# Attention and feed-forward on one core: the hand-written order redone from tile 0's last chunks on, with part of VectorE's work on GpSimd

## The chip, the cores and the metric

The kernel runs on one core of a Trainium2 chip. The metric is device time in microseconds (us) of one execution. Each time given for a kernel is the median of its runs. The traces come from one profiled execution each.

A core has five engines with an instruction queue each: TensorE (PE) multiplies matrices, VectorE (DVE), ScalarE (ACT) and GpSimd (POOL) work element by element, and SyncE (SP) issues transfers. Each engine runs its queue strictly in program order. An instruction that waits for another engine or a transfer holds up all that is queued behind it.

## The reference

Causal linear attention with a decay per head, and behind it a SwiGLU feed-forward block. B=4, H=8, S=768, D=64; 3072 tokens of width 512; the inner width d_ff is 1536. All inputs and the output are fp32.

```python
for b in range(nb):                       # blocks of 64 positions, state kv carried along
    intra = einsum('bhic,bhjc->bhij', qb, kb) * Dmask
    intra = einsum('bhij,bhjd->bhid', intra, vb)
    inter = einsum('bhid,bhde->bhie', qb * lam_pow, kv_state)
    out[:, :, sl] = intra + inter
    kv_state = lam_block * kv_state + einsum('bhsd,bhse->bhde', kb * rev_pow, vb)
x = out.transpose(0, 2, 1, 3).reshape(3072, 512)
g = x @ w_gate
result = (g * sigmoid(g) * (x @ w_val)) @ w_out
```

## The kernel before

Matmuls run in bf16. The attention works in 12 **groups** g, each one batch and a pair of blocks of 128 positions, all heads. Two groups make a **tile** t of 512 tokens, and there are six tiles for the feed-forward. The inner width is cut into 12 chunks fc of 128.

What a group goes through, with the names of the helpers and the lines on which they issue:
- `load_fp32` fetches k, q and v (L109; from group 6 on L116 and L124, in four pieces for q and for k and two for v). SP issues these transfers.
- `kcast` (L278) and `qcast` (L282, it also multiplies the decay in) write k and q as bf16 into one tile `qk`; `v_scale` (L260) does the same for v, with the decay factors.
- `dma_transpose` (L268) turns the whole `qk` into `qkt` by a transfer on SP. It needs both casts. From group 3 on all groups use it.
- `scores` (L347, from group 6 on L383) and `mask` (L358, L362, on DVE) make the block's own weights; `intra` (L554) and `inter` (L541) make the output in a pair of PSUM banks, from the block and from the state; `guard` (L525) reads that pair on ACT between the two; `evr` (L569, L572) copies it to `xt`, the input of the feed-forward.
- `upd_mm` (L408) makes the update of the state from k and v. `sadd` (L489), `kvm` (L508), `kv0c` (L513), `kvf0`, `kvz` and `kvn` (L443, L445) add it, decay it and copy it to bf16 for the next blocks.

The feed-forward: tiles 0 to 2 take `ffn_gate` (L600, with silu on ACT in L605) and `ffn_val` (L618, with the product on DVE in L622) for a chunk and all or half of the tile's tokens. Tiles 3 to 5 use Strassen's method in Winograd's form: `unit` holds six PSUM banks, `uprod` (L755) is one of its seven products for gate or value, with sums on ACT and DVE (L759 to L765), then `silu` (L774) and `mu` or `mup` (L780). The sums of weights and inputs that it needs come from `w_combo` (L680) and `x_combo` (L719). The last product takes `ffn_out` for tile 0, and for the other tiles `oprod` (L814, sums in L817 to L829), seven products likewise, whose sums of inputs come from `hsum` (L673) and `wo_combo` (L658). `wo_cast` (L254) makes bf16 of w_out.

The order on every engine is written out by hand as a list of several hundred such calls; there is no scheduler (`tc.manual_schedule()`). The arguments name the engine where there is a choice (`nc.gpsimd` or `POOLC` is POOL, `nc.vector` or `DVEC` is DVE, `ACTC` is ACT), and `use(...)` names the PSUM banks (0 to 7) that the next call takes. A call whose bank is still being read waits. From the list, around the first changed place:

```python
    kcast(3)
    qcast(3, nc.gpsimd)
    dma_transpose(3)
    load_fp32(4, nc.sync, v, "v")
    use(6); ffn_gate(0, 11, 2, 4)
    use(7); ffn_val(0, 11, 2, 4)
    v_scale(3, nc.gpsimd)
    v_scale(4, nc.gpsimd)
```

The arguments of a matmul call are the tile, the chunk and the half of the tile's tokens (`0, 2` or `2, 4`; `0, 4` is the whole).

Of the kernel before, what the change touches and what calls it, by code (L numbers as in the profile page):

```python
# [37 lines left out]
def _body(ctx, tc, nc, q, k, v, lam, moe_w_gate, moe_w_val, moe_w_out, out):  # L38
# [896 lines left out]
    def use(*bk):  # L935
        fixed[:] = bk
# [40 lines left out]
    use(2, 3, 4, 5); scores(2)  # L977
    mask(2, 0, 0)
    mask(2, 0, 1)
    mask(2, 1, 0)  # L980
    mask(2, 1, 1)
    use(6); ffn_gate(0, 10, 0, 4)
    use(7); ffn_val(0, 10, 0, 4)
    use(0); ffn_gate(0, 11, 0, 2)
    use(1); ffn_val(0, 11, 0, 2)
    use(2, 3); upd_mm(2)
    kvz(2)
    kvf0(2)
    use(4, 5); op_bare(2)
# [3 lines left out]
    evr(2, 0, DVEC)  # L993
    evr(2, 1, ACTC)
    sadd(2, 1)
# [12 lines left out]
    new_xt(2)  # L1008
    use(0); ffn_gate(1, 0, 0, 2)
    use(1); ffn_val(1, 0, 0, 2)  # L1010
    use(2); ffn_gate(1, 1, 0, 2)
    use(3); ffn_val(1, 1, 0, 2)
    use(4); ffn_gate(1, 2, 0, 2)
    use(5); ffn_val(1, 2, 0, 2)
    use(6); ffn_gate(1, 3, 0, 2)
    use(7); ffn_val(1, 3, 0, 2)
    kcast(4)
    qcast(4, nc.vector)
# [8 lines left out]
    use(0); ffn_gate(1, 4, 0, 2)  # L1027
    use(1); ffn_val(1, 4, 0, 2)
    use(2); ffn_gate(1, 5, 0, 2)
    use(3); ffn_val(1, 5, 0, 2)  # L1030
    use(4); ffn_gate(1, 6, 0, 2)
    use(5); ffn_val(1, 6, 0, 2)
    use(6); ffn_gate(1, 7, 0, 2)
    use(7); ffn_val(1, 7, 0, 2)
    use(0, 1, 2, 3); scores(3)
    use(4, 5); upd_mm(3)
    mask(3, 0, 0)
    mask(3, 1, 1)
    mask(3, 0, 1)
    mask(3, 1, 0)  # L1040
    use(2, 3); op_new(3)
    kvz(3)
    use(6); ffn_gate(1, 8, 0, 2)
    use(7); ffn_gate(1, 9, 0, 2)
    use(0); ffn_gate(1, 10, 0, 2)
    inter(3, True)
    guard(3)
    use(6); ffn_gate(1, 11, 0, 2)
    kvf0(3)
    intra(3, False)  # L1050
    use(0, 6); upd_mm(4)
    sadd(3, 1)
    sadd(4, 0)
    use(1); ffn_val(1, 10, 0, 2)
    evr(3, 1, ACTC)
    evr(3, 0, ACTC)
    use(4); ffn_val(1, 11, 0, 2)
    kvm(3, nc.vector)
    use(5); ffn_val(1, 8, 0, 2)
    use(7); ffn_val(1, 9, 0, 2)  # L1060
    use(3); ffn_gate(1, 0, 2, 4)
    kcast(5, ACTC)
    use(5); ffn_gate(1, 1, 2, 4)
    qcast(5, nc.vector)
    use(0); ffn_gate(1, 2, 2, 4)
    kvn(4, 0, ACTC)
    use(7); ffn_gate(1, 3, 2, 4)
    sadd(4, 1)
    use(1); ffn_val(1, 0, 2, 4)
    use(3); ffn_val(1, 1, 2, 4)  # L1070
    use(5); ffn_gate(1, 4, 2, 4)
    use(4); ffn_gate(1, 5, 2, 4)
    kvm(4, nc.vector)
    use(2); ffn_val(1, 2, 2, 4)
    use(7); ffn_val(1, 3, 2, 4)
    use(1); ffn_gate(1, 6, 2, 4)
    use(5); ffn_val(1, 6, 2, 4)
    use(6); ffn_gate(1, 7, 2, 4)
    use(1); ffn_val(1, 5, 2, 4)
    use(4, 3, 2, 6); scores(4)  # L1080
    mask(4, 0, 0)
    mask(4, 1, 0)
    v_scale(5, nc.gpsimd)
    wo_cast()
    wo_cast()
# [4 lines left out]
    use(0, 7); op_new(4)  # L1090
    inter(4, True)
    mask(4, 0, 1)
    use(1); ffn_val(1, 4, 2, 4)
    mask(4, 1, 1)
    use(4); ffn_gate(1, 8, 2, 4)
    guard(4)
    use(5); ffn_gate(1, 9, 2, 4)
    use(2); ffn_gate(1, 10, 2, 4)
    use(4); ffn_val(1, 10, 2, 4)
    use(1); ffn_val(1, 8, 2, 4)  # L1100
    intra(4, False)
    use(4, 2); upd_mm(5)
    new_xt(3)
    evr(4, 0, ACTC)
    evr(4, 1, ACTC)
    use(6); ffn_val(1, 7, 2, 4)
    sadd(5, 0)
    use(3); ffn_val(1, 9, 2, 4)
    use(0); ffn_gate(1, 11, 2, 4)
    kvn(5, 0, ACTC)  # L1110
    use(1); ffn_gate(2, 6, 0, 2)
    wo_cast()
    wo_cast()
    wo_cast()
    sadd(5, 1)
    use(5); ffn_gate(2, 7, 0, 2)
    use(6); ffn_val(1, 11, 2, 4)
    use(4); ffn_val(2, 6, 0, 2)
    wo_cast(ACTC)
    use(7); ffn_out(0, 0)  # L1120
    use(6); ffn_gate(2, 8, 0, 2)
    wo_combo(0)
    wo_combo(1)
    w_combo(0, 0, (0, 3))
    w_combo(1, 0, (0, 3))
    kvm(5, nc.vector)
    use(2); ffn_val(2, 8, 0, 2)
    use(7); ffn_val(2, 7, 0, 2)
    use(4); ffn_gate(2, 9, 0, 2)
    use(3); ffn_out(0, 1)  # L1130
    kcast(6, ACTC)
    qcast(6, nc.gpsimd)
    use(0, 2); op_new(5)
    use(7, 5, 4, 6); scores(5)
    inter(5, True)
    dma_transpose(6)
    load_fp32(7, nc.sync, k, "kraw")
# [40 lines left out]
    out_new(1, (0,), [4, 6, 0], 0)  # L1178
    mask(6, 0, 1)
    use(5); ffn_val(2, 9, 2, 4)  # L1180
    sadd(6, 0)
    w_combo(0, 1, (0, 3))
    mask(6, 0, 0)
    oprod(1, 0, 1)
    kv0c(5, ACTC)
    use(5); ffn_gate(2, 10, 0, 4)
    oprod(1, 0, 7)
    kvn(6, 0, ACTC)
    sadd(6, 1)
    oprod(1, 0, 6)  # L1190
    kvn(6, 1, ACTC)
    sadd(6, 2)
    use(2); ffn_gate(2, 11, 0, 4)
    kvn(6, 2, ACTC)
    sadd(6, 3)
    use(1); ffn_val(2, 8, 2, 4)
    w_combo(1, 1, (0, 3))
    oprod(1, 0, 5)
    oprod(1, 0, 2)
    use(2); ffn_gate(2, 0, 0, 4)  # L1200
    use(3); ffn_val(2, 0, 0, 4)
    use(1); ffn_val(2, 11, 0, 4)
    w_combo(0, 3, (0, 3))
    w_combo(0, 2, (0, 3))
    use(5); ffn_val(2, 10, 0, 4)
    oprod(1, 0, 3)
    use(4); ffn_gate(2, 1, 0, 4)
    oprod(1, 0, 4)
    store(1, 0, 1, 0, 512, None)
    store(1, 0, 0, 0, 512, None)  # L1210
    use(1, 3); op_new(6)
    inter(6, True)
    use(2, 5); upd_mm(7)
    use(6, 4); scores(7)
    guard(6)
    intra(6, False)
    w_combo(1, 2, (0, 3))
    evr(6, 1, ACTC)
    kcast(8, ACTC)
    mask(7, 0, 0)  # L1220
    hsum(1, 1, 0, 6, 1, 2, nc.vector)
    mask(7, 0, 1)
    use(7); ffn_val(2, 1, 0, 4)
    sadd(7, 0)
    kvm(6, nc.vector)
# [5 lines left out]
    out_new(1, (1,), [0, 7, 4], 0)  # L1231
    kv0c(3, ACTC)
    use(3); ffn_gate(2, 2, 0, 4)
    evr(6, 0, ACTC)
    use(6); ffn_gate(2, 3, 0, 4)
    oprod(1, 1, 1)
    use(3); ffn_val(2, 2, 0, 4)
    kvn(7, 0, ACTC)
    sadd(7, 1)
    oprod(1, 1, 7)  # L1240
    kvn(7, 1, ACTC)
    sadd(7, 2)
    oprod(1, 1, 6)
    oprod(1, 1, 2)
    kvn(7, 2, ACTC)
    use(1); ffn_gate(2, 4, 0, 4)
    oprod(1, 1, 4)
    sadd(7, 3)
    v_scale(8, nc.vector, 0, 4)
    v_scale(8, nc.gpsimd, 4, 8)  # L1250
    w_combo(1, 3, (0, 3))
    kvm(7, nc.vector)
    oprod(1, 1, 5)
    use(4, 3); op_new(7)
    inter(7, True)
    use(5, 2); upd_mm(8)
    use(1, 0); scores(8)
    mask(8, 0, 1)
    sadd(8, 0)
    guard(7)  # L1260
    intra(7, False)
    evr(7, 1, ACTC)
    evr(7, 0, ACTC)
    kv0c(4, ACTC)
    kv0c(6, ACTC)
    kvn(8, 0, ACTC)
    sadd(8, 1)
    kvn(8, 1, ACTC)
    use(6); ffn_gate(2, 5, 0, 4)
    v_scale(9, nc.gpsimd, 0, 4)  # L1270
    sadd(8, 2)
    x_combo(3, 0, None, nc.vector)
    x_combo(3, 1, None, nc.vector)
    x_combo(3, 3, None, nc.vector)
    use(0); ffn_val(2, 4, 0, 4)
    mask(8, 0, 0)
    x_combo(3, 2, None, nc.vector)
    use(5); ffn_val(2, 3, 0, 4)
    kvn(8, 2, ACTC)
    hs_new(2)  # L1280
    new_xt(4)
    unit(3, 0, (2, 4, 3, 1, 6, 5))
    uprod(3, 0, 0, 0)
    uprod(3, 0, 1, 0)
    kcast(9, ACTC)
    uprod(3, 0, 0, 1)
    oprod(1, 1, 3)
    uprod(3, 0, 1, 1)
    uprod(3, 0, 3, 0)
    silu(3, 0, 0, 0)  # L1290
    qcast(9, nc.vector)
    uprod(3, 0, 2, 0)
    use(0); ffn_val(2, 5, 0, 4)
# [5 lines left out]
    use(2, 0); op_new(8)  # L1299
    uprod(3, 0, 2, 1)  # L1300
    uprod(3, 0, 4, 0)
    uprod(3, 0, 5, 0)
    inter(8, True)
    uprod(3, 0, 3, 1)
    mu(3, 0, 0, 0)
    hsum(2, 0, 0, 4, 0, 2, nc.vector)
    uprod(3, 0, 6, 0)
    guard(8)
    silu(3, 0, 1, 1)
    silu(3, 0, 1, 0)  # L1310
    silu(3, 0, 0, 1)
# [417 lines left out]
```

## Time and profile before

| | |
|---|---|
| time, median of 3 runs | 214.70 us (214.65 to 215.71) |
| the profiled execution | 215.46 us, of which its trace spans 213.5 us |
| granted TensorE clock in it | 0.998 of full speed |
| instructions | 6988 |

The trace covers 213.5 of the profiled execution's 215.46 us; the rest lies before the first instruction and behind the last. In the profile's rows a line such as L282 is the line of the helper that issued the instruction, so one line stands for all groups and a row's start tells which group it is. In a timeline, a row gives the start in us, the duration in us, engine, line, operation, output and input by the program's names, and how many instructions of one kind stand in it; the bracket at the end is the engine's idle time just before it and what ended that. SPq and POOLq are the queues of these engines, with the transfers that they issue.

### The profile page before, as it was taken

How to read it: one execution, taken by the hardware profiler on the slowest of the kernel's cores; microseconds unless marked ns; L12 is line 12 of the kernel's file. 1: busy time of each engine (PE TensorE's matmuls, PEld its weight loads, DVE VectorE, ACT ScalarE, POOL GpSimd, SP SyncE). 2: the span in 40 equal slices, each digit the busy share in tenths (PEclk: the TensorE clock that was granted, in tenths of full speed). 3: DMA queues.
4: the chain of work that ended last, by engine and by line, in shares of the span. 5: the costliest groups of instructions: out<-in, count | busy, mean ns of one | idle time of the engine just before them, and what ended most of it. 6: DMA issues, size and time to landing. Idle time of an engine off the chain costs nothing.

```text
span 213.5 us, 6988 instructions
## 1 busy us (share of the span) xinstructions
PE 206.1 (97%) x2873; PEld 160.4 (75%) x2873; DVE 158.7 (74%) x304; ACT 133.1 (62%) x287; POOL 72.4 (34%) x92
## 2 busy tenths in 40 slices
PE   8799999999999999999899999999999999999993
PEld 3466455888886648876667888888888888888883
DVE  1774447678678898986898999979896779953960
ACT  6888575656635444838578986657763577527522
POOL 6685755705362030640103289802000000006600
PEclk9999999999999999999999999999999999999999
DMA  6999999989999967999777858972000500005014
GB/s 189 344 354 382 377 355 282 306 224 250 284 392 156 225 195 166 267 171 226 204 198 173 196 128 197 274 219 107 5 3 0 196 3 0 3 0 196 3 51 147
DMA packets 82177, 39.77 MB, mean 186 GB/s; under 512 B 45410, under 2 KB 77794, under 8 KB 82146
## 3 DMA queue, kind: packets, MB, share of 16 engines
q1 hardware_dynamic: 80946, 38.74, 66.4%
q10 hardware_dynamic: 1200, 0.59, 0.9%
q8 instruction: 22, 0.36, 0.7%
q14 instruction: 9, 0.07, 0.1%
HBM read 28.31 MB, written 6.29 MB: 162 GB/s over the span
## 4 chain that ended last, share of the span: by engine, by line
PE 68%; SPq 13%; DMA 10%; POOL 3%; issue 2%; ACT 2%; DVE 1%; POOLq 0%; DVEq 0%
PE bank L755 25%; PE bank L814 17%; PE bank L600 10%; PE bank L618 10%; DMA qraw<-in_q_dram 6%; SPq L124 6%; DMA v<-in_v_dram 3%; SPq L116 3%; SPq L109 3%; POOL qk L282 2%; SPq L268 2%; PE bank L554 2%; PE bank L541 1%; PE bank L408 1%; POOL v_s L260 1%
## 5 line engine op out<-in xcount | busy, mean ns | idle before, releaser
L622 DVE TENSOR_TENSOR h<-sil,bank 128x256 bf16<-128x256 bf16 (+1 forms) x55 | 26.9, 500 | 17.4 <-PE bank L618 13.1
L618 PE MATMUL bank<-xt,wv_sb 128*128 128x256 bf16 (+1 forms) x228 | 38.4, 301 | 0.1
L600 PE MATMUL bank<-xt,wg_sb 128*128 128x256 bf16 (+1 forms) x228 | 38.2, 301 | 0.0
L605 ACT ACTIVATE sil<-bank 128x256 bf16<-128x256 f32 (+1 forms) x55 | 24.5, 451 | 18.2 <-PE bank L600 14.8
L260 POOL TENSOR_TENSOR v_s<-v,dec 128x512 bf16<-128x512 f32 (+1 forms) x15 | 19.8, 1328 | 36.1 <-DMA v<-in_v_dram 35.9
L618 PEld LDWEIGHTS <-wv_sb 128*128 128x128 bf16 x228 | 21.8, 98 | 9.3 <-issue 0.4
L600 PEld LDWEIGHTS <-wg_sb 128*128 128x128 bf16 x228 | 21.7, 98 | 8.5 <-issue 0.2
L814 PEld LDWEIGHTS <-h 128*128 128x128 bf16 x240 | 23.4, 98 | 4.6 <-issue 1.1
L755 PEld LDWEIGHTS <-ws 128*128 128x128 bf16 x216 | 20.9, 98 | 3.1 <-issue 0.5
L814 PE MATMUL bank<-wo_sb,h 128*128 128x256 bf16 x180 | 22.4, 273 | 0.0
L755 PE MATMUL bank<-xs,ws 128*128 128x256 bf16 x144 | 20.7, 272 | 0.2 <-ACT bank L759 0.2
L780 DVE TENSOR_TENSOR h<-sil,bank 128x512 bf16<-128x512 bf16 x27 | 18.2, 681 | 1.8 <-PE bank L755 1.5
L814 PEld LDWEIGHTS <-hs 128*128 128x128 bf16 x180 | 17.6, 98 | 2.2
L774 ACT ACTIVATE sil<-bank 128x512 bf16<-128x512 f32 x27 | 15.7, 594 | 5.2 <-PE bank L755 5.0
L673 POOL TENSOR_TENSOR hs<-h,hs 128x512 bf16<-128x512 bf16 x2 | 2.3, 1152 | 46.4 <-DVE hs L673 46.3
L362 DVE TENSOR_TENSOR ssb<-bank,causal 128x512 bf16<-128x512 f32 x24 | 15.2, 682 | 2.0 <-PE bank L347 1.2
L763 DVE TENSOR_TENSOR bank<-bank,es 128x512 f32<-128x512 f32 x18 | 12.3, 696 | 5.9 <-PE bank L755 5.5
L755 PE MATMUL bank<-xt,wg_sb 128*128 128x256 bf16 x108 | 15.9, 273 | 0.2 <-DVE kvf L489 0.2
L755 PE MATMUL bank<-xt,wv_sb 128*128 128x256 bf16 x108 | 16.1, 273 | 0.0
L755 PEld LDWEIGHTS <-wg_sb 128*128 128x128 bf16 x144 | 14.0, 98 | 2.3 <-issue 0.4
L814 PE MATMUL bank<-wt,hs 128*128 128x256 bf16 x120 | 15.5, 272 | 0.0
L755 PEld LDWEIGHTS <-wv_sb 128*128 128x128 bf16 x144 | 13.9, 98 | 1.7
(133 smaller groups left out, 373.4 us busy)
## 6 DMA issues: line engine op xcount, KB each, us to landing
out_dram<-osb SPq DMA_DIRECT2D x22, 256.0 KB, 2.3
v<-in_v_dram SPq DMA_DIRECT2D x18, 256.0 KB, 4.6
woraw<-in_moe_w_out_dram SPq DMA_DIRECT2D x6, 512.0 KB, 7.7
kraw<-in_k_dram SPq DMA_DIRECT2D x24, 128.0 KB, 3.6
qraw<-in_q_dram SPq DMA_DIRECT2D x24, 128.0 KB, 3.4
wraw<-in_moe_w_gate_dram SPq DMA_DIRECT2D x5, 512.0 KB, 6.9
wraw<-in_moe_w_val_dram SPq DMA_DIRECT2D x5, 512.0 KB, 6.8
kraw<-in_k_dram SPq DMA_DIRECT2D x4, 512.0 KB, 6.6
```

The source lines that it names most:

```text
L124: eng.dma_start(out=t[p0:p0 + n, :, s * D:s * D + D], in_=bass.AP(tensor=src.tensor, offset=base + (H - 1) * S * D * rev + (p0 + s * BLK) * D,
L260: eng.tensor_tensor(out=st[("vs", g)][:, h0:h1], in0=st[("v", g)][:, h0:h1].rearrange("p h (s d) -> p h s d", s=2), in1=vfac(g, h0, h1), o ...
L362: nc.vector.tensor_tensor(out=st[("ssb", g)][:, h2, 2 * c:2 * c + 2].rearrange("p a s n -> p a (s n)"), in0=st[("sp", g, c, h2)].rearrange ...
L600: nc.tensor.matmul(gp[:, n0:n1], wg_sb[:, mc, fs], xt[:, g0:g1, mc].rearrange("p g b n -> p g (b n)"), start=(mc == 0 and n0 == 0), stop=( ...
L605: nc.scalar.activation(sil[:, 0:N], gp[:, 0:N], AF.Silu)
L618: nc.tensor.matmul(vp[:, n0:n1], wv_sb[:, mc, fs], xt[:, g0:g1, mc].rearrange("p g b n -> p g (b n)"), start=(mc == 0 and n0 == 0), stop=( ...
L622: nc.vector.tensor_tensor(out=h_sb[:, fc % FH, b0:b1].rearrange("p b n -> p (b n)"), in0=sil[:, 0:N], in1=vp[:, 0:N], op=ALU.mult)
L755: nc.tensor.matmul(o[i][:, fi * 256:fi * 256 + 256], lhs(c, 2 * j + fi), rhs(c), start=(k < 2 and fi == 0 and c == 0), stop=(c == KH - 1), ...
L763: nc.vector.tensor_tensor(out=E[i], in0=Bb[i], in1=es[i], op=ALU.add)
L774: nc.scalar.activation(sil[half, r], unit_src(t, j, half, r)[0], AF.Silu)
L780: eng.tensor_tensor(out=st[("h", t, half)][:, 2 * j:2 * j + 2][:, :, r:B:2], in0=v3(st[("u", t, j)][4][half, r]), in1=v3(unit_src(t, j, ha ...
L814: nc.tensor.matmul(o, lhs(f), rhs(f), start=(k in (1, 7) and f == 0), stop=(f == FH - 1), skip_group_check=True)
```

## The change

The list of calls is written anew from tile 0's last three chunks on, up to some way into unit (5,2) of the last tile; the calls behind that and the helpers are the same. The same matmuls are issued, in another order and with other PSUM banks. SP issues the same transfers in the same order. On the engines:
- From DVE to POOL: `qcast(4)`, `qcast(5)`, `kvm(3)` to `kvm(7)`, `v_scale(6)`, half of `v_scale(8)`, half of `v_scale(11)`, five `x_combo` (of tiles 3, 4 and 5), four `mup` (of units (4,0) to (5,0)) and several `hsum` of tiles 2 to 4; two `hsum` go the other way.
- Between ACT and POOL: `kv0c(2)` and `kvn(11,1)` to ACT, or back to it; `kcast(10)`, `kvn(6,1)` and `kvn(8,1)` to POOL.
- `qcast` of groups 3, 6, 7, 10 and 11 is on POOL in both kernels, and that of 8 and 9 on DVE in both.

In the diff, cut to the parts around groups 3 to 5, around groups 8 and 9, and one of the later parts:

```diff
     kcast(3)
+    use(3); ffn_val(1, 0, 0, 2)
+    use(0); ffn_gate(1, 3, 0, 2)
+    v_scale(3, nc.gpsimd)
     qcast(3, nc.gpsimd)
     dma_transpose(3)
     load_fp32(4, nc.sync, v, "v")
-    use(6); ffn_gate(0, 11, 2, 4)
-    use(7); ffn_val(0, 11, 2, 4)
-    v_scale(3, nc.gpsimd)
...
+    use(7, 0); upd_mm(3)
...
+    kcast(4)
...
+    qcast(4, nc.gpsimd)
+    kvm(2, nc.gpsimd)
+    kvm(3, nc.gpsimd)
     v_scale(4, nc.gpsimd)
-    kvm(2, nc.gpsimd)
-    kv0c(2, POOLC)
     load_fp32(5, nc.sync, k, "kraw")
     load_fp32(5, nc.sync, q, "qraw")
...
-    qcast(4, nc.vector)
+    use(3, 0); op_new(3)
+    inter(3, True)
+    use(4, 7, 2, 1); scores(3)
...
     v_scale(5, nc.gpsimd)
     wo_cast()
-    wo_cast()
+    qcast(5, nc.gpsimd)
     dma_transpose(5)
     load_fp32(6, nc.sync, k, "kraw")
     load_fp32(6, nc.sync, q, "qraw")
...
     kcast(7, POOLC)
+    kvm(4, nc.gpsimd)
+    kvm(5, nc.gpsimd)
     qcast(7, nc.gpsimd)
...
     qcast(8, nc.vector)
     dma_transpose(8)
     load_fp32(9, nc.sync, k, "kraw")
     load_fp32(9, nc.sync, q, "qraw")
     load_fp32(9, nc.sync, v, "v")
...
+    oprod(1, 1, 6)
...
-    use(4, 3); op_new(7)
+    use(2, 1); op_new(7)
     inter(7, True)
-    use(5, 2); upd_mm(8)
-    use(1, 0); scores(8)
+    guard(7)
+    use(5, 6); scores(8)
+    use(7, 0); upd_mm(8)
+    intra(7, False)
...
+    kcast(9, ACTC)
...
+    use(6); ffn_val(2, 3, 0, 4)
...
-    use(7, 4); upd_mm(9)
-    use(3, 6); scores(9)
+    use(7, 0); upd_mm(9)
+    evr(8, 0, ACTC)
+    evr(8, 1, ACTC)
     uprod(3, 0, 5, 1)
...
+    use(1, 3); scores(9)
...
-    kcast(10, ACTC)
-    qcast(10, nc.gpsimd)
+    kcast(10, POOLC)
+    qcast(10, nc.gpsimd)
```

More of the change, by code (lines that the diff above doesn't have):

```diff
@@ new lines, in _body @@
+    hsum(1, 0, 0, 6, 1, 2, nc.vector)
+    use(1); ffn_val(2, 7, 0, 2)
+    oprod(1, 0, 1)
+    evr(5, 1, ACTC)
+    oprod(1, 0, 7)
+    use(4); ffn_gate(2, 9, 0, 2)
+    w_combo(0, 1, (0, 3))
+    oprod(1, 0, 6)
+    hsum(1, 2, 0, 6, 1, 2, nc.vector)
+    use(1); ffn_gate(2, 6, 2, 4)
+    hsum(1, 3, 0, 6, 1, 2, nc.vector)
+    use(2); ffn_val(2, 9, 0, 2)
+    use(4); ffn_gate(2, 7, 2, 4)
+    oprod(1, 0, 4)
+    use(1, 4); upd_mm(6)
+    use(2, 3); scores(6)
+    sadd(6, 0)
+    use(5); ffn_val(2, 6, 2, 4)
@@ L1209, in _body @@
+    use(5); ffn_gate(2, 1, 0, 4)
+    use(5, 3); op_new(6)
+    kvm(6, nc.gpsimd)
+    v_scale(7, nc.gpsimd)
+    v_scale(8, nc.gpsimd, 0, 4)
+    v_scale(8, nc.gpsimd, 4, 8)
+    use(6); ffn_val(2, 11, 0, 4)
+    inter(6, True)
+    guard(6)
+    use(2, 7); upd_mm(7)
+    use(1, 0); scores(7)
+    intra(6, False)
     store(1, 0, 1, 0, 512, None)
     store(1, 0, 0, 0, 512, None)
[L1211 to L1216, printed above, removed]
@@ L1217, in _body @@
-    w_combo(1, 2, (0, 3))
+    evr(6, 0, ACTC)
+    sadd(7, 0)
+    mask(7, 0, 0)
+    out_new(1, (1,), [6, 4, 5], 0)
+    oprod(1, 1, 1)
+    kcast(8, ACTC)
+    use(1); ffn_gate(2, 2, 0, 4)
+    oprod(1, 1, 7)
+    kvn(7, 0, ACTC)
+    w_combo(0, 3, (0, 3))
+    sadd(7, 1)
+    kvn(7, 1, ACTC)
     evr(6, 1, ACTC)
-    kcast(8, ACTC)
-    mask(7, 0, 0)
-    hsum(1, 1, 0, 6, 1, 2, nc.vector)
+    w_combo(0, 2, (0, 3))
     mask(7, 0, 1)
-    use(7); ffn_val(2, 1, 0, 4)
-    sadd(7, 0)
-    kvm(6, nc.vector)
+    sadd(7, 2)
@@ L1280, in _body @@
+    use(5); ffn_val(2, 5, 0, 4)
     hs_new(2)
     new_xt(4)
-    unit(3, 0, (2, 4, 3, 1, 6, 5))
+    unit(3, 0, (7, 0, 1, 2, 3, 5))
+    uprod(3, 0, 0, 1)
+    use(4); ffn_val(2, 4, 0, 4)
+    use(6); ffn_val(2, 3, 0, 4)
+    qcast(9, nc.vector)
     uprod(3, 0, 0, 0)
+    kv0c(7, ACTC)
     uprod(3, 0, 1, 0)
-    kcast(9, ACTC)
-    uprod(3, 0, 0, 1)
-    oprod(1, 1, 3)
     uprod(3, 0, 1, 1)
+    uprod(3, 0, 2, 0)
+    uprod(3, 0, 3, 1)
+    uprod(3, 0, 2, 1)
     uprod(3, 0, 3, 0)
     silu(3, 0, 0, 0)
-    qcast(9, nc.vector)
@@ L1292, in _body @@
-    uprod(3, 0, 2, 0)
-    use(0); ffn_val(2, 5, 0, 4)
+    uprod(3, 0, 4, 0)
+    mu(3, 0, 0, 0)
+    v_scale(9, nc.gpsimd, 0, 4)
     v_scale(9, nc.gpsimd, 4, 8)
```

724 lines of the change are left out of this document (337 added, 387 removed).

## The prediction

> **What bounds the kernel now.** I read the page first, then TensorE's timeline, then the chain of waits.
>
> ```profile
> span 213.5 us, 6988 instructions
> PE 206.1 (97%) x2873; PEld 160.4 (75%) x2873; DVE 158.7 (74%) x304; ACT 133.1 (62%) x287; POOL 72.4 (34%) x92
> ```
>
> TensorE (PE) is busy for 206.1 of 213.5 us. The change issues the same matmuls, so it can only win what PE loses, some 7 us, much of it ahead of the first redone statement. PE's timeline shows what is lost behind that. Matmul rows overlap, so I measure from one row's start to the next one's start.
>
> ```profile
> 97.93 1.89 PE L600 MATMUL bank<-xt,wg_sb 128*128 128x512 bf16 x8
> 99.65 0.82 PE L814 MATMUL bank<-wo_sb,h 128*128 128x256 bf16 x6
> ...
> 103.13 1.03 PE L600 MATMUL bank<-xt,wg_sb 128*128 128x512 bf16 x4
> 105.02 0.81 PE L814 MATMUL bank<-wt,h 128*128 128x256 bf16 x6 [0.86 <-DVE bank L823]
> ...
> 106.78 0.44 PE L408 MATMUL bank<-v_s,qk 64*64 64x64 bf16 x24
> 107.15 0.44 PE L383 MATMUL bank<-qkt 64*64 64x64 bf16 x32
> ...
> 108.67 2.14 PE L618 MATMUL bank<-xt,wv_sb 128*128 128x512 bf16 x8
> 110.64 1.04 PE L755 MATMUL bank<-xt,wg_sb 128*128 128x256 bf16 x8
> ...
> 114.00 1.03 PE L618 MATMUL bank<-xt,wv_sb 128*128 128x512 bf16 x4
> 115.20 1.03 PE L755 MATMUL bank<-xs,ws 128*128 128x256 bf16 x8 [0.18 <-ACT bank L759]
> ...
> 119.32 0.61 PE L755 MATMUL bank<-xs,ws 128*128 128x256 bf16 x4
> 120.11 0.60 PE L755 MATMUL bank<-xt,wg_sb 128*128 128x256 bf16 x4 [0.19 <-DVE kvf L489]
> 120.55 0.60 PE L755 MATMUL bank<-xt,wv_sb 128*128 128x256 bf16 x4
> ```
>
> Unhindered, eight matmuls of 512 columns take 1.72 us (97.93 to 99.65), so four take 0.86; four of 256 take 0.44 (120.11 to 120.55). Against that PE loses 1.03 us at 105.02 (1.89 less 0.86; the row itself says 0.86 idle), 0.25 within the eight at 108.67 (1.97 less 1.72), 0.34 at 115.20 and 0.35 at 119.32. That is nearly 2 us of the 2.8 or so that I find lost in the whole redone stretch; the rest are single losses under 0.3. From 125 us on PE is paced by its matmuls almost throughout. So the gain has a ceiling of less than 3 us, and a loss has none.
>
> What causes the largest of these losses stands in the chain of waits, from the 60s to 105 us. It is not PE's work, but a loop through SP, the queue that issues loads and transposes (start, us, what):
>
> ```profile
> 75.74 1.92 POOL qk L282
> 77.67 1.65 SPq L268
> ...
> 88.53 1.91 POOL qk L282
> 90.46 1.91 SPq L268
> ...
> 96.79 5.00 DMA qraw<-in_q_dram
> ```
>
> The q of a group lands, its cast (L282) runs, the transpose of k and q (L268) starts on SP the moment that the cast ends (75.74 and 1.92 make 77.66), and the next group's loads are queued behind it on SP. Then the next q lands, and so on. A delay anywhere in the loop is carried to the next group. SP's own timeline shows that there is no air in it:
>
> ```profile
> 33.64 1.42 SPq L109 DMA_DIRECT2D v<-in_v_dram  x1
> ...
> 40.46 3.12 SPq L268 DMA_TRANSPOSE qkt<-qk  x1
> ...
> 44.88 1.47 SPq L109 DMA_DIRECT2D qraw<-in_q_dram  x1
> 46.51 5.48 SPq L268 DMA_TRANSPOSE qkt<-qk  x1
> ...
> 57.32 8.48 SPq L268 DMA_TRANSPOSE qkt<-qk  x1
> ...
> 103.38 1.69 SPq L268 DMA_TRANSPOSE qkt<-qk  x1
> ```
>
> A transpose with nothing outstanding holds SP for 1.65 to 1.69 us. Those at 40.46, 46.51 and 57.32 (groups 3, 4, 5) hold it for 3.12, 5.48 and 8.48, until the loads ahead of them have landed. These rows leave SP no slack.
>
> **The change, part by part.** PE's set of matmuls and SP's order are the same. What moves is the order on PE, ACT, DVE and POOL, and some 25 operations from DVE to POOL. Of q's casts, it is 4 and 5 that go from DVE to POOL; 8 and 9 stay on DVE.
>
> *Group 3's cast on POOL.* The order of `qcast(3)` and `v_scale(3)` is turned round: the scale now comes first. POOL runs its queue in order, so the cast cannot begin until v of group 3 has landed and been scaled. POOL's timeline of before, then the landing time of the v load issued at 33.64, then that of the transposes:
>
> ```profile
> 38.30 1.91 POOL L282 TENSOR_TENSOR qk<-qraw,dec 128x1024 bf16<-128x1024 f32 x1 [1.59 <-DVE h L622]
> 40.17 1.92 POOL L260 TENSOR_TENSOR v_s<-v,dec 128x1024 bf16<-128x1024 f32 x1
> ...
> 49.88 0.62 POOL L508 TENSOR_TENSOR kvs<-kvf,lamgrp 128x256 f32<-128x256 f32 x1
> ```
>
> ```profile
> DMA to landing us min/median/max: 6.1/6.1/6.1
> ```
>
> ```profile
> DMA to landing us min/median/max: 3.7/3.7/5.1
> ```
>
> The load issued at 33.64 lands at 39.75. The scale then runs from about 39.85 for 1.92 and the cast for 1.91, to 43.7. The transpose starts there. It holds SP for 1.65 instead of 3.12, because its loads will have landed: SP is free at 45.4 where it was at 43.58 (40.46 and 3.12). **Shift of the loop: +1.8 us.**
>
> First price of that: transpose 3 lands at 43.7 and 3.7, 47.4. PE asks for it for `inter(3)`, which the change puts ahead of `scores(3)`:
>
> ```profile
> 46.62 0.64 PE L347 MATMUL bank<-qkt 64*64 64x128 bf16 x32
> 47.09 0.42 PE L408 MATMUL bank<-v_s,qk 64*64 64x64 bf16 x32
> 47.44 1.48 PE L600 MATMUL bank<-xt,wg_sb 128*128 128x256 bf16 x12
> ```
>
> By the diff one half chunk fewer (0.44) and the group's state update (0.35, 47.09 to 47.44) stand ahead of it, so PE is there at 46.62 less 0.44 plus 0.35, 46.5, and waits 0.9. It isn't added to the sum: it only takes up time that PE would spend waiting for group 8 later.
>
> *The loop from 45 to 102 us.* Transposes 4 and 5 are held by loads issued behind transpose 3, so they move with it; the casts of groups 4 and 5 on POOL end before those loads land, so the slower POOL costs nothing there. The cover is SP's hold, 5.48 and 8.48 us. Groups 6 and 7 move by the same 1.8. Two state scalings (`kvm`, 0.62 each on POOL) now stand between group 7's k cast and q cast on POOL; they fit into its wait for q, and cost at most 0.15 by my layout. The cast of group 8 stays on DVE:
>
> ```profile
> 102.01 1.23 DVE L282 TENSOR_TENSOR qk<-qraw,qdn 128x1024 bf16<-128x1024 f32 x1 [2.10 <-DMA qraw<-in_q_dram]
> ...
> 104.54 0.43 DVE L823 TENSOR_TENSOR bank<-bank,osb 128x256 f32<-128x256 f32 x1
> ```
>
> It starts at 102.01 plus 1.9, ends at 105.1, and the transpose starts at 105.25 instead of 103.38 and lands at 109.0. While DVE waits for q, everything behind it on DVE waits too: before, that was the product (L622) and the bank sum at 104.54 that PE waited for at 105.02. In the new order it is the sum of `oprod(1,1,6)`, so the same kind of stall returns about 1.1 us long. It too lies inside the wait for group 8.
>
> *Where it is paid.* `scores(8)` needs transpose 8. It started at 107.15, as the transpose landed (103.38 and 3.7). Now it starts at 109.0: **+1.85**. The change also puts `scores(8)` ahead of `upd_mm(8)`, so the update's 0.37 (106.78 to 107.15), done before the wait until now, comes behind it: **+0.37**.
>
> *What goes.* Behind that point the new order removes three losses. `ffn_val(2,3)` gets a bank that is long free (0.25 at 108.67); `kcast(9)` no longer stands in ACT's queue ahead of the copies that free a bank (0.34 at 115.20); a product of unit (3,0) stands between update and scores of group 9 (0.35 at 119.32). **-0.94**, if nothing is late in their place; if all three come back in another form, 0. The losses ahead of 107.15 don't count, since that point is set by the loop.
>
> *Behind 121 us.* Group 9's transpose is issued at about 120.2 on my layout, a little ahead of its use; groups 10 and 11 have room. Sums moved to POOL fall into empty time:
>
> ```profile
> 150.00:170.00 20.00, 20.00 (x241) 17.73 (x230) 16.09 (x33) 12.69 (x28) 0.00 (x0) 1.00 0.14 54
> ```
>
> In this row of the windows POOL (the fifth pair) does nothing and PE never stops, while DVE is busy for 16.09 of 20. POOL's slower sums are due a microsecond or more ahead of their readers. I take 0, with 0.3 to either side.
>
> **Sum:** 1.85 + 0.37 - 0.94 = +1.3. The profiled execution took 215.46, so it would take 216.7; the median of the three runs is 214.7, 0.76 lower, and gives **216.0**. The bounds: the shift may be 1.1 (the loads queued behind it find idle DMA engines and land sooner) to 2.6 (transpose 3 lands after 5.1, the longest in the row above, and the cast is late as well), and what goes may be 0: 215.2 to 217.6.
>
> **The rivals.**
>
> *The shift grows at the POOL casts (0.17).* A POOL operation can be slowed by what DVE does, and the reverse:
>
> ```profile
> 90.39 2.63 POOL L260 TENSOR_TENSOR v_s<-v,dec 128x1024 bf16<-128x1024 f32 x1
> ```
>
> ```profile
> 76.52 1.54 DVE L673 TENSOR_TENSOR hs<-hs,h 128x768 bf16<-128x768 bf16 x1
> 77.98 0.55 DVE L673 TENSOR_TENSOR hs<-h,hs 128x768 bf16<-128x768 bf16 x1
> ```
>
> The same scale took 1.92 at 40.17 and 2.63 here; the same sum took 0.55, and 1.54 beside the POOL cast at 75.74. The new order gives POOL more to do beside DVE's sums in this stretch. Were the casts of groups 6 and 7 each hit by 0.71, the loop would be late by another 1.4: 217.4. Against it: in before the casts themselves took 1.90 to 1.92 each time, and DVE was the one that paid. The Trainium skill ("SBUF — State Buffer", "Who interferes with whom") says that a VectorE instruction with two inputs in SBUF contends with a GpSimd instruction that reads SBUF, and that whoever issues second blocks. The rows above agree, in both directions.
>
> *The loop catches up, and the change is faster (0.20).* If DMA is the limit rather than SP's order (loads waiting long in filled queues would land as they did), transposes 4 to 8 come as before and only the stalls go. Break-even is a shift at group 8 of 0.94 less 0.37, about 0.6 us: below that it gains. With no shift left, 1.03 and 0.94 go: 212.7. With transpose 3's 0.9 added and half of the 0.94 back in another form it is 214.1. For it: SP's holds of 5.48 and 8.48 us are waits for landings. Against it: from 66 to 103 us each row of the loop starts where the one before it ends, so there what is late stays late.
>
> *Half of it stays (0.13).* The shift is worn down to about 1 us: +1.0 + 0.37 - 0.94, near 215.1, between 214.3 and 215.3.
>
> **How the numbers follow.** The loop carried whole has 0.50; its own range is 215.2 to 217.6. The measurement can tell about 0.5%, 1.07 us: from 213.6 to 215.8 it counts as the same. Of the first case nearly two thirds lie above (0.32), of the growing shift all (0.17) and of the half shift and the misses of my layout a few hundredths: slower 0.53. Faster takes three quarters of the catching-up case: 0.15. The same has the rest, 0.32. The range reaches from 213.2, in the middle of the catching-up case, to 217.8, just past the growing shift; what is left out is about 0.1 on each side.
>
> **What would show it.** In the changed kernel's profile: on POOL, a scale (L260) at about 39.9 and the cast (L282) behind it at 41.8; on SP, the transpose at 43.7; on PE, an idle of nearly 1 us at `inter(3)` (L541), ended by the DMA of qkt; transposes on SP near 79.5, 92.3 and 105.2; `scores(8)` (L383) at 109.0, ended by the DMA of qkt; no gap of 0.3 between 110 and 122. I am wrong if the transpose at 77.67 comes before 78.5, or if `scores(8)` starts without a wait for its transpose. I am wrong on the sum if PE shows gaps behind 125 us.

## The result, and the profile after

| | before | changed |
|---|---|---|
| median | 214.68 us (214.60 to 215.71, 4 runs) | 217.81 us (217.53 to 218.77, 4 runs) |
| profiled execution, its span | 215.46, 213.5 us | 217.62, 215.9 us |

The ratio is 1.0143, with a 95% interval of 1.0098 to 1.0187: slower, by 3.1 us in the medians. In the experiments, where before has a median of about 215.9 us, the changed kernel has 1.0110 (1.0073 to 1.0148). All ratios below are against before measured together with it on the same chip; 0.1% is 0.2 us.

The page of the changed kernel: PE does the same work, DVE is relieved and POOL loaded, as the change says.

```profile
span 215.9 us, 6996 instructions
PE 207.3 (96%) x2870; PEld 161.1 (75%) x2873; DVE 150.6 (70%) x278; ACT 133.0 (62%) x286; POOL 103.7 (48%) x119
```

The start of the predicted chain, in the timelines of POOL and then of SP: v's scale first, the q casts behind it, and the transposes of groups 3, 6 and 8.

```profile
39.51 1.91 POOL L260 TENSOR_TENSOR v_s<-v,dec 128x1024 bf16<-128x1024 f32 x1 [3.12 <-DMA v<-in_v_dram]
41.38 3.92 POOL L282 TENSOR_TENSOR qk<-qraw,dec 128x1024 bf16<-128x1024 f32 x2
```

```profile
43.32 1.74 SPq L268 DMA_TRANSPOSE qkt<-qk  x1
...
77.53 1.65 SPq L268 DMA_TRANSPOSE qkt<-qk  x1
...
102.93 1.68 SPq L268 DMA_TRANSPOSE qkt<-qk  x1
```

Transpose 3 comes at 43.32, 2.9 us later than in before. But in this execution transposes 6 and 8 come at 77.53 and 102.93, a little earlier than the 77.67 and 103.38 of before. PE's timeline has these rows with idle time of its own behind the first redone statement:

```profile
47.27 0.30 PE L541 MATMUL bank<-qkt,kvn 64*64 64x128 bf16 x4 [0.22 <-DMA qkt<-qk]
...
51.87 0.45 PE L408 MATMUL bank<-v_s,qk 64*64 64x64 bf16 x32 [0.45 <-POOL v_s L260]
...
114.10 0.61 PE L755 MATMUL bank<-xs,ws 128*128 128x256 bf16 x4 [0.16 <-ACT bank L759]
...
119.97 0.60 PE L755 MATMUL bank<-xt,wg_sb 128*128 128x256 bf16 x4 [0.17 <-DVE kvf L489]
...
127.40 0.60 PE L755 MATMUL bank<-xt,wg_sb 128*128 128x256 bf16 x4 [0.27 <-DVE h L780]
128.58 0.60 PE L755 MATMUL bank<-xs,ws 128*128 128x256 bf16 x4 [0.58 <-ACT bank L759]
...
136.06 0.22 PE L554 MATMUL bank<-ssb,v_s 64*64 64x64 bf16 x3 [0.95 <-issue]
```

Measured from start to start against the pace of the matmuls, they lose 0.39, 0.66, 0.33, 0.36, 0.43, 0.74 and 1.14 us, 4.05 together. Two of them, 0.33 and 0.36, are those of before at 115.20 and 120.11 over again. Gone are before's 1.03 at 105.02 and its 0.25 near 109.8. So 3.36 us are new and 1.28 are gone, 2.08 net; the spans differ by 2.4 and the two profiled executions by 2.16. Three of the new ones, 2.31 us together, lie behind 121 us, where the prediction had put nothing.

One profile is one execution. A second profile of each kernel, both from one chip, shows a late transpose 8. SP of before and then of the changed kernel, transposes 3 and 8:

```profile
40.74 2.83 SPq L268 DMA_TRANSPOSE qkt<-qk  x1
...
101.88 2.54 SPq L268 DMA_TRANSPOSE qkt<-qk  x1
```

```profile
44.01 1.75 SPq L268 DMA_TRANSPOSE qkt<-qk  x1
...
104.21 1.67 SPq L268 DMA_TRANSPOSE qkt<-qk  x1
```

And PE of the changed kernel there:

```profile
107.98 0.45 PE L383 MATMUL bank<-qkt 64*64 64x64 bf16 x32 [0.51 <-DMA qkt<-qk]
...
137.29 0.22 PE L554 MATMUL bank<-ssb,v_s 64*64 64x64 bf16 x3 [0.83 <-issue]
```

Transpose 8 is 2.3 us later than in before there, and `scores(8)` waits for it. But transpose 6 is only 0.6 us later (78.44 against 77.81), so the shift is not carried evenly along the loop. The stop in the middle of `intra(9)` is there again, before the same three matmuls.

Divided at the start of `scores(8)`, where the prediction put the price, the profiles say where the time goes. Up to there the changed kernel takes 106.72 and 107.98 us in its two profiles, before 107.15 and 106.55. From there to the end of the span it takes 109.2 and 109.3, before 106.4 and 106.7: some 2.7 us more, in both pairs.

### The profile page after: what moved, and what is told of

It reads as the page before. It is cut to its first block, busy times and chain, and to the rows that moved or that the text cites. A ratio compares the mean times of both kernels' runs of the same rounds, so it can differ in the third digit from the quotient of the medians.

```text
span 215.9 us, 6996 instructions
## 1 busy us (share of the span) xinstructions
PE 207.3 (96%) x2870; PEld 161.1 (75%) x2873; DVE 150.6 (70%) x278; ACT 133.0 (62%) x286; POOL 103.7 (48%) x119
## 4 chain that ended last, share of the span: by engine, by line
PE 72%; DMA 11%; POOL 6%; SPq 4%; issue 3%; DVE 3%; ACT 1%; POOLq 0%; ACTq 0%; DVEq 0%
PE bank L755 24%; PE bank L814 22%; PE bank L618 8%; PE bank L600 8%; DMA wraw<-in_moe_w_val_dram 6%; PE bank L638 5%; DMA v<-in_v_dram 4%; POOL v_s L260 4%; SPq L109 3%; PE bank L554 2%; PE bank L541 1%; PE bank L408 1%; DVE hs L673 1%; POOL wv_sb L243 1%; POOL qk L282 1%
## 5 line engine op out<-in xcount | busy, mean ns | idle before, releaser
L600 PE MATMUL bank<-xt,wg_sb 128*128 128x256 bf16 (+1 forms) x228 | 37.7, 301 | 0.0
L260 POOL TENSOR_TENSOR v_s<-v,dec 128x512 bf16<-128x512 f32 (+1 forms) x18 | 24.1, 1355 | 26.2 <-DMA v<-in_v_dram 16.2
L780 POOL TENSOR_TENSOR h<-sil,es 128x512 bf16<-128x512 bf16 x9 | 10.8, 1203 | 13.8 <-DVE es L765 13.0
```

The costliest lines, as they stand in the source:

```text
L260: eng.tensor_tensor(out=st[("vs", g)][:, h0:h1], in0=st[("v", g)][:, h0:h1].rearrange("p h (s d) -> p h s d", s=2), in1=vfac(g, h0, h1), o ...
L600: nc.tensor.matmul(gp[:, n0:n1], wg_sb[:, mc, fs], xt[:, g0:g1, mc].rearrange("p g b n -> p g (b n)"), start=(mc == 0 and n0 == 0), stop=( ...
L780: eng.tensor_tensor(out=st[("h", t, half)][:, 2 * j:2 * j + 2][:, :, r:B:2], in0=v3(st[("u", t, j)][4][half, r]), in1=v3(unit_src(t, j, ha ...
```

## The experiments

| run | edit | ratio to before, 95% interval |
|---|---|---|
| after_again | the changed kernel | 1.0110 (1.0073 to 1.0148) |
| e1_q_first | q cast of group 3 first | 1.0021 (0.9989 to 1.0054) |
| e7_q_and_k_first | and its k cast earlier | 1.0021 (0.9992 to 1.0050) |
| e2_hsum_pool | one sum back to POOL | 1.0102 (1.0067 to 1.0137) |
| e3_code_shift | instruction blocks shifted | 1.0085 (1.0050 to 1.0120) |
| e9_scores_early | scores(10) earlier | 1.0077 (1.0048 to 1.0106) |
| e6_q_and_hsum | e1 and e2 | 1.0024 (0.9996 to 1.0052) |
| e5_all_three | e1, e2 and e3 | 1.0065 (1.0032 to 1.0097) |
| e8_best | e7, e2 and e9 | 1.0020 (0.9999 to 1.0041) |
| e10_repaired | e8 and three more | 0.9995 (0.9963 to 1.0028) |
| e4_before_v_first | before, v's scale first | 1.0059 (1.0034 to 1.0085) |
| before_again | before | 1.0003 (0.9973 to 1.0033) |

**The two kernels again.**

> The kernel before, unchanged, for a second profile on the chip of the other runs. All theories expect the same time as before. On the first profile transposes 3 and 8 started at 40.46 and 103.38; if loads land later on this chip, the transposes come later here as well, and the 1.03 us loss at oprod's bank sum near 105 is larger.

> The changed kernel, unchanged, for a second profile and a time on this chip. Theory B (SP's loop carries the lateness of transpose 3, as predicted; the first profile of the changed kernel, where transpose 8 came at 102.93, was a lucky one): transpose 8 is issued 1.5 to 2 us later than in the kernel before on this chip, PE waits for it at scores(8), and the ratio is 1.010 to 1.016. Theory A (the loop has caught up by group 6): transposes 6 to 8 start within 0.3 us of those of before, there is no wait at scores(8), and the loss lies at 47, 52, 127 and 136 alone.

Their rows are shown above. The second expectation's theory B held on the ratio, on the wait at `scores(8)` and on transpose 8 (2.3 us late; 1.5 to 2 were expected). What differs between the two executions of one kernel is how long q's loads take to land. In before, the last piece of group 8's q was issued at 96.79 and took 5.00 us; in the second profile of before it was issued at 96.85 and took 3.34. So transpose 8 moved by 1.5 us with nothing changed. The scatter of a single landing is as large as the shift that the prediction was about.

**The q cast first.**

```diff
-    v_scale(3, nc.gpsimd)
     qcast(3, nc.gpsimd)
+    v_scale(3, nc.gpsimd)
```

> The changed kernel with qcast(3) put back ahead of v_scale(3) on POOL; nothing else differs. In the changed kernel PE loses 0.39 us at inter(3) (47.27, ended by the transpose) and 0.66 at the state update of group 4 (51.87, ended by v_scale(4)), whose v load is queued behind transpose 3 on SP. Theory A (both come from the turned order): transpose 3 starts at about 41.5 on SP instead of 43.3, both gaps go, and the time falls by 0.7 to 1.05 us, to about 216.9. Theory B, the prediction's (the lateness is carried by SP's loop to group 8): transposes 6 to 8 come 1.8 us earlier too, and more than 1.05 us is won. Theory C (the early gaps are refilled later by the stalls that PE now skips): under 0.3 us is won.

The ratio falls by 0.9%, some 1.9 us; the two intervals together leave 0.4 to 1.4%, 0.9 to 3 us. Theory C is out. The best value is nearly twice the 1.05 us of the two early gaps, which is theory B's side, but A's 1.05 is just inside. The next run makes the same turn in the other kernel. The profiled execution of this one took 220.52 us, 4.5 above the median, so only its times are used.

**The same in the kernel before.**

```diff
+    v_scale(3, nc.gpsimd)
     qcast(3, nc.gpsimd)
     dma_transpose(3)
 ...
-    v_scale(3, nc.gpsimd)
```

> The kernel before with v_scale(3) put ahead of qcast(3) on POOL; nothing else differs. Theory A, the prediction's (SP's loop carries the lateness of transpose 3 to group 8): transpose 8 is issued about 1.5 to 1.8 us later than 103.38 and the time rises by 1.2 to 1.9 us. Theory B (loads wait in filled DMA queues until about 66 us, so transposes 6 to 8 come as before): PE loses 0.4 to 0.6 at scores(3), perhaps 0.6 at the update of group 4, and gets most of it back at 105, where it waited 1.03 us in the kernel before: the time rises by 0 to 0.4 us.

Slower by 0.59%, 1.27 us, at the low end of theory A and well above the 0.4 us of B (the interval begins at 0.34%, 0.7 us). The transposes of groups 3 and 8 on SP, and what PE waited for:

```profile
43.79 1.75 SPq L268 DMA_TRANSPOSE qkt<-qk  x1
...
106.12 1.68 SPq L268 DMA_TRANSPOSE qkt<-qk  x1
```

```profile
47.73 0.64 PE L347 MATMUL bank<-qkt 64*64 64x128 bf16 x32 [0.78 <-DMA qkt<-qk]
...
52.51 0.44 PE L408 MATMUL bank<-v_s,qk 64*64 64x64 bf16 x32 [1.01 <-POOL v_s L260]
...
107.76 0.82 PE L814 MATMUL bank<-wt,h 128*128 128x256 bf16 x6 [1.31 <-DVE bank L823]
```

The early waits are there, and the wait at the bank sum behind the q cast of group 8, 0.86 in the first profile of before and nothing in the second, did not shrink to make up for them: it is 1.31. The lateness was carried, not made up. The size is read from the times: the profiled execution, 218.33 us, is the slowest of its twelve (median 217.16), and its transpose 8, 2.7 us later than in the first profile of before, is later than the times bear out.

**The k cast as well.**

```diff
     evr(2, 0, ACTC)
+    kcast(3)
     use(2); ffn_gate(1, 0, 0, 2)
     use(7); ffn_gate(1, 1, 0, 2)
     use(5); ffn_gate(1, 2, 0, 2)
-    kcast(3)
```

> The changed kernel with qcast(3) ahead of v_scale(3) on POOL and, besides, kcast(3) on ACT put back right behind evr(2,0), ahead of the first three gate chunks of tile 1. With the q cast first alone, transpose 3 started at 42.9, as the k cast on ACT ended (41.82 and 1.04), and not at 40.7 as in the kernel before. Theory A (two late casts, of which each alone holds transpose 3): transpose 3 starts at 40.6 to 41.2, its wait at inter(3) goes, and the ratio to before falls from the 1.0021 of the q cast first to between 0.997 and 1.001. Theory B (transposes 4 to 8 are set by when loads land, whatever transpose 3 does): transpose 3 comes 2 us sooner, but transposes 6 and 8 and the ratio stay within 0.15% of the q cast first.

With the q cast first alone (here in the kernel that also has its sum on POOL), the transpose still waited, for the k cast on ACT. ACT and SP of that kernel, then SP of this one:

```profile
41.82 1.04 ACT L278 CAST qk<-kraw 128x1024 bf16<-128x1024 f32 x1
```

```profile
42.94 1.75 SPq L268 DMA_TRANSPOSE qkt<-qk  x1
```

```profile
40.38 3.20 SPq L268 DMA_TRANSPOSE qkt<-qk  x1
```

Both casts were late, each enough to hold the transpose; the prediction had seen only one. Repairing the second moved transpose 3 by 2.6 us, took its wait at `inter(3)` away, and brought nothing that the times can tell (1.0021 both times). Theory B's bound held for the ratio. In this execution transposes 6 and 8 came at 76.93 and 103.41, against 77.85 and 103.55 there: of the 2.6 us, 0.9 and 0.1 were left. In e8 below, which repairs both casts too, they came at 76.60 and 102.03, 1.2 and 1.5 earlier than there. So how much of an earlier start arrives differs from one execution to the next, and what sets it was not tried; in the times nothing of it shows, for e8 has 1.0020.

**The sum beside the cast.**

```diff
-    hsum(2, 0, 4, 6, 0, 2, nc.vector)
+    hsum(2, 0, 4, 6, 0, 2, nc.gpsimd)
```

> The changed kernel with one sum, hsum(2,0,4,6), back on POOL as before the change; it stays at its place in the list. In the changed kernel this sum takes 1.80 us on DVE at 124.95, beside the cast of q (L282) that POOL starts at 124.56, where its shape takes 0.42 alone; PE then loses 0.43 at 127.40 and 0.74 at 128.58. Theory A (DVE is held by the POOL cast, and the products L780, the silu behind them and the bank copies L759 come late): both gaps go and 0.9 to 1.2 us is won. Theory B (the gaps come from the new order of ACT and DVE in this unit, the sum only fills a wait): less than 0.3 us is won.

DVE and POOL of the changed kernel around the two gaps, and the group of before with this sum's shape (mean in ns behind the comma):

```profile
124.95 1.80 DVE L673 TENSOR_TENSOR hs<-h 128x512 bf16<-128x512 bf16 x1
126.67 1.27 DVE L780 TENSOR_TENSOR h<-sil,bank 128x512 bf16<-128x512 bf16 x2
```

```profile
124.56 1.90 POOL L282 TENSOR_TENSOR qk<-qraw,qdn 128x1024 bf16<-128x1024 f32 x1 [0.77 <-DVE bank L763]
```

```profile
L673 DVE TENSOR_TENSOR hs<-h 128x512 bf16<-128x512 bf16 x6 | 2.5, 418 | 0.1
```

A sum of 0.42 us takes 1.80 and ends 0.3 us after the cast on POOL (126.75 against 126.46); the cast itself takes its usual 1.90. This agrees with the rule cited in the prediction from the Trainium skill ("SBUF — State Buffer", "Who interferes with whom"): two SBUF inputs on VectorE, GpSimd reading, and the one that comes second blocks. With the sum on POOL both gaps behind it are gone from PE's timeline. The time is not: 1.0102 against 1.0110, and the same between e6 and e1 (1.0024 against 1.0021), where 0.4 to 0.6% was to be won; the intervals of each pair leave about 0.5% to either side. In the profile the gaps' time is won: from `scores(8)` to the end of the span it takes 107.7 us, 1.5 less than in the changed kernel's two profiles. But in this execution `scores(8)` waited until 109.02 for its transpose, issued at 105.26, so it was late before that point.

One reason why the times show so little stands in other profiles. In e7 above and in e3 and e9 below, where this sum is still on DVE, it started at 125.15, 127.43 and 125.41 and the cast on POOL at 125.15, 127.60 and 125.94. There the sum was no later than the cast and took 0.42, 0.42 and 0.41, and neither gap is in PE's timeline. DVE and POOL of e7:

```profile
125.15 0.42 DVE L673 TENSOR_TENSOR hs<-h 128x512 bf16<-128x512 bf16 x1
```

```profile
125.15 2.18 POOL L282 TENSOR_TENSOR qk<-qraw,qdn 128x1024 bf16<-128x1024 f32 x1 [0.63 <-DMA qraw<-in_q_dram]
```

So the gaps come from the sum where the cast is first, and which of the two is first differs from one execution to the next. In what share of the executions it is the cast, the profiles can't tell, nor what the sum costs on average.

**PE without instructions.** PE's instructions come to it in blocks of 16 KB. The trace shows each as one transfer on a queue of its own, 22 of them in an execution.

```diff
-    for _ in range(4):
-        nc.tensor.matmul(b, warm[:, 0:128], warm, start=True, stop=True)
+    nc.tensor.matmul(b, warm[:, 0:128], warm, start=True, stop=True)
+    for _ in range(32):
+        nc.tensor.matmul(b[0:64, 0:64], warm[0:64, 0:64], warm[0:64, 0:64], start=True, stop=True)
```

> The changed kernel with three of PE's warm-up matmuls of 512 columns at the very start replaced by 32 small ones (64 x 64 x 64): 29 matmuls more in the program, the same work behind them, and no order changed. In the changed kernel PE stands still for 1.14 us at 136.06 in the middle of intra(9), for nothing that the profile shows, 258 PE instructions after the 16 KB instruction block whose transfer starts at 133.01. Theory A (PE ran out of instructions, because four groups of small matmuls stand in a row and use up a block in 2 us, faster than the next one comes): the blocks' borders move by 58 instructions against the program, the next block is asked for earlier, and the 1.14 us gap at intra(9) goes or shrinks below 0.3; the time falls by 0.8 to 1.1 us unless another border falls on such a row. Theory B (a data or bank dependence that the profile does not show, or chance of that one execution): the gap stays, or goes without any change of the time.

The stop in `intra(9)` is gone, with no change in order, data or banks near it. The ratio fell by 0.25% only, less than theory A had and within what the intervals leave open; this execution lost 2.22 us at `inter(3)` and 0.77 at `scores(11)`, both ended by transposes, and the small matmuls cost up to 0.4 us at the start.

```diff
+    use(2, 7); scores(10)
     uprod(3, 2, 5, 0)
 ...
-    use(0, 2); op_new(9)
+    use(0, 3); op_new(9)
 ...
-    use(3, 7); scores(10)
```

> The changed kernel with scores(10) alone put ahead of uprod(3,2,5,0) (other banks, no other edit). Theory A (PE ran out of instructions in a row of four groups of small matmuls): 64 PE instructions less stand between the asking for the next block and its need there, PE is busy 3 us longer with it, and the 0.9 to 1.14 us gap in intra(9) goes although no border is moved; the ratio falls by about 0.4% below the 1.011 of the changed kernel on this chip, to 1.005 to 1.009. Theory B (the gap belongs to intra(9) itself, a bank or data that the profile does not show): it stays.

The stop is gone here too, and the ratio is 1.0077, 0.33% less, inside theory A's range (the two intervals overlap). The profiled execution is the second fastest of nine (216.17, median 217.31), and the two gaps at the sum are missing in it as well, so its time is not that of an execution without the stop alone. And in the next kernel, e8, with the same place edited, it is back. PE of e8:

```profile
133.56 0.42 PE L554 MATMUL bank<-ssb,v_s 64*64 64x64 bf16 x29
134.78 0.22 PE L554 MATMUL bank<-ssb,v_s 64*64 64x64 bf16 x3 [0.80 <-issue]
```

What differs most is how long the transfer of the instruction block takes. The DMA view of a stretch names the queue that brings PE's instructions (packets, MB, share of 16 engines' time). In order, the changed kernel from 133.0 to 134.6, e8 from 131.7 to 133.4, e9 from 132.3 to 133.3:

```profile
q8 instruction: 1, 0.02, 6.2%
```

```profile
q8 instruction: 1, 0.02, 5.9%
```

```profile
q8 instruction: 1, 0.02, 5.6%
```

16 engines times the stretch times the share is 1.59, 1.60 and 0.90 us for one block of 16 KB. By the packets' own times it lasts from 133.01 to 134.59 in the changed kernel, and PE goes on at 136.06, 1.47 later. In six executions with the stop (the changed kernel twice, e2, e6, e7, e8) PE goes on 1.42 to 1.56 us after the end of this block's transfer, whose own length is 0.88 to 1.61, and always with the same three matmuls. From the transfer's start it is 2.3 to 3.1, so the end of the transfer is what PE follows. In e9 the block ends at 133.25, so PE could go on at about 134.7 or 134.8; it reaches these three at 134.9, 1.6 us after the block's end, where in e8 it stood before them 0.4 after it. Of these 1.2 us, 0.7 is the length of the transfer; the rest is that e8's block was asked for later against PE's work. That is the same rule with the other outcome. So the cause of the stop is shown: PE has run out of instructions. In the changed order it needs the block's 256 or so instructions in about 2 us, because inter, scores, update and intra, 240 instructions of loads and matmuls, stand in a row; in before the row is broken by a product of 0.44 us, and its block took 0.88. The Trainium skill ("Runtime: NRT & Kernel Launch", "Instruction fetch mechanics") has the 16 KB blocks of 256 instructions, fetched while the one before is executed; there the fetch counts as hidden, since instructions are dispatched more slowly than they come. The rows do not agree with that for small matmuls, at 32 in 0.28 us.

**Together.**

> The changed kernel with qcast(3) ahead of v_scale(3) and hsum(2,0,4,6) on POOL, without the shift of the instruction blocks. If PE's stop in intra(9) is the supply of instructions, it stays here, 0.9 to 1.1 us near 135, and this kernel is slower than the one with all three edits by as much (0.4 to 0.5%). If it was something else that the shift only happened to hide, the two agree within 0.2%.

The stop stayed, 1.12 us at 135.10, as a lack of instructions would have it. The second half failed: the kernel with all three edits was not faster than this one but slower.

> The changed kernel with all three edits: qcast(3) ahead of v_scale(3), hsum(2,0,4,6) back on POOL, and the 29 extra small warm-up matmuls at the start that move the borders of PE's instruction blocks. If the three losses are separate (about 1.2% for the turned order with what SP carries, 0.5% for the sum beside the POOL cast, 0.5% for the instruction supply), the ratio to before is 0.99 to 0.998. If they hide each other (what one gives back is lost at the next wait), it stays at the 1.002 of the first edit alone.

1.0065. No stop in `intra(9)` in its trace, but 1.57 us at `inter(3)`, 0.79 at 117.2 for a sum on DVE, and 0.62 at `scores(11)` for its transpose. Whether the shift at the start brings these or the execution did, one profile can't tell. The price of the stop in the times therefore rests on e9 alone, with the limits named there.

> The changed kernel with four edits: qcast(3) and kcast(3) early, hsum(2,0,4,6) on POOL, and scores(10) put ahead of uprod(3,2,5,0) (banks 2 and 7, with op_new(9) on 0 and 3), so that four groups of small matmuls no longer stand in a row on PE. If the losses are separate: no gap at inter(3), none at 127 to 129, none in intra(9), and a ratio of 0.990 to 0.997, faster than the kernel before. If what they give back is lost at the waits for transposes 8 and 11, 0.998 to 1.002.

1.0020: the second alternative by the ratio, though its profile shows the stop (0.99) where none was expected.

> The changed kernel with the four edits of e8 and three more: upd_mm(8) ahead of scores(8), so that the update fills part of the wait for transpose 8; upd_mm(10) with its sums moved behind intra(9) and oprod(2,1,1), so that the row of small matmuls is broken twice; hsum(2,3,4,6) on DVE moved behind the sums of oprod(2,1,6) and oprod(2,0,6), which PE waited for at 139.9 in e8. If the gaps are separate and PE is the bound between the waits of SP's loop: no stop in intra(9) (0.99 in e8), no gap near 140 (0.41), 1.2 to 1.5 us less than e8, a ratio of 0.993 to 0.998, faster than the kernel before. If the loop sets the time: the gaps go, waits for transposes 8 to 11 come in their place, and the ratio stays at 0.999 to 1.003.

0.9995 (0.9963 to 1.0028): the second alternative, as fast as before and not faster. The stop and the gap near 140 are gone. `scores(8)` waits again for transpose 8, issued at 105.09, in an execution that was the slowest of its twelve (218.13, median 216.08) and late already ahead of the first edited statement.

The stretch from `scores(8)` to the end of the span sets these profiles side by side. With the stop and the gaps at the sum (the changed kernel twice) it takes 109.2 and 109.3 us. With the stop alone (e2, e6, e7) it takes 107.7 to 107.8, and with neither (e3, e5, e9, e10) 107.0 to 108.1; before has 106.4 and 106.7. e8 doesn't fit: with the stop and a few waits of its own it takes 109.0, from a `scores(8)` that began at 105.81, earlier than in any other. Single executions can't be priced closer than this.

The two readings are not at one. The times put 0.9% on the turned order, the profiles most of the loss behind `scores(8)`. e7, with the order put back and the sum left on DVE, is 0.8 us ahead of the second profile of the changed kernel at `scores(8)` and gains 1.5 us more from there to the end, where it lacks the gaps at the sum. So part of what the order gives back may come through the sum. Whether the order decides which of sum and cast is first was not tried.

## Why the prediction was right or wrong

**Right.** The chain of the first part. The scale ahead of the cast was to be at 39.9 and the cast at 41.8; they were at 39.51 and 41.38. The transpose was due at 43.7 and came at 43.32 and 44.01. The wait at `inter(3)` was to be 0.9: 0.39 and 0.78. Transpose 8 was due at 105.25 and `scores(8)` at 109.0: 102.93 without a wait in the first profile, 104.21 and 107.98 in the second, 105.26 and 109.02 in e2. Transpose 9, which the prediction had at about 120.2, was issued at 114.63 and 115.64; 120.2 is about where its landing would have been, and nothing hung on it. Undoing the turned order gives 0.9% (0.4 to 1.4%), about the 1.85 us that the sum had for it, and doing it alone in the kernel before costs 1.27 us. The test that the prediction had set itself, "wrong if the transpose at 77.67 comes before 78.5", was failed by the first profile (77.53) and, by a hair, the second (78.44): it took the landing of loads as fixed, where it moves by more than a microsecond from one execution to the next. The other test, gaps behind 125 us, found three.

**Wrong, by its own steps.** The size: +1.3 was forecast, +3.1 measured (+2.4 by the second ratio). That 217.81 still meets the upper end of the range, 217.8, is luck: the range went that far for a shift that grows, and what filled it are the losses behind 121 us. From `scores(8)` on, the prediction's terms (+0.37, -0.94 and 0) make the new order 0.57 us shorter; the profiles have it 2.7 us longer.
- *"Behind 121 us ... I take 0, with 0.3 to either side."* This is the term that was mis-sized. It measured 0.43 and 0.74 in PE's rows behind the sum, and 1.14 for the stop, of which the times bear out some 0.7 us for the stop (e9, with overlapping intervals) and nothing certain for the sum. The step looked at what moves from DVE to POOL into empty time. It did not look at the sum that goes the other way, on to DVE beside a cast on POOL (`hsum(2,0,4,6)`; the two kernels have this one, not two), nor at how many small matmuls the new order puts in a row.
- *"What goes: -0.94."* Only the 0.25 went. Before the row at 114.10 ACT still has `kcast(9)` (it merely starts at 111.20) and a state copy ahead of the bank copies; 0.33 was lost there, 0.34 before. Between update and scores of group 9 a product does stand now, but the state sums on DVE that release the bank come as late: 0.36 instead of 0.35. That is 0.69 too much in the sum.
- *Transpose 3 alone on POOL's account.* The k cast on ACT was late as well. It changed no number, since the q cast was later still, but undoing the one would not have been enough to undo the shift of transpose 3.
- *The 0.37 of the update behind `scores(8)`* can't be told from the scatter of transpose 8.

**The rivals.** The shift did not grow at the POOL casts: those of groups 3 to 10 took 1.90 to 1.92 in both profiles. The port did cost, at another place, and DVE paid. The loop that catches up was what the first profile shows; the kernel was slower all the same, by the losses behind 121 us, which stand in both of its profiles, with transpose 8 late or not. That half of the shift stays can't be ruled out. Transpose 8 came at 104.3 on average in five profiles with the turned order (the changed kernel twice, e2, e3 and e9), at 103.5 in five with the q cast first (e5 to e8 and e10) and at 102.6 in the two of before; but single ones of a kind lie up to 3.1 us apart.

## What to carry to other kernels

Where one engine is 96% busy and its order is written by hand, a reordering is read by what it puts ahead of the transfers: two operations turned round on a half-idle engine cost 0.6 to 0.9% through a queue that issues loads behind a waiting transpose. A prediction from one profile should say how far the landings in it scatter, and price operations moved to an engine by what runs on the engine that shares its port. And a long row of very short matmuls has a price of its own, the supply of instructions, which no wait in the profile names: look for idle time put down to issue, at the same instruction in each execution that has it.

## What the hardware showed that was not expected

PE stopped for 0.8 to 1.14 us in rows of 176 to 240 instructions of small matmuls, the longer of them within about 1.2 us, and went on 1.42 to 1.56 us after its next 16 KB block of instructions had been transferred; the transfer itself took 0.88 to 1.61 us beside other loads. The landing of one 128 KB load of q took 3.3 us in one execution and 5.0 in another, at the same place of the same program; the times of the kernel before, 214.4 to 217.1 us in one set of runs, spread as widely, though no run here ties the one to the other.
